# Ten x tiles loaded at once, wv and the last two tiles behind the fourth tile's transpose, one output add on GpSimd

## The chip, the core and the metric

The kernel runs on one core of a Trainium2 chip. The core has TensorE (PE) with its weight loads (PEld), VectorE (DVE), ScalarE (ACT), GpSimd (POOL) and SyncE (SP), whose queue issues all DMAs of this kernel. Each engine works through its own queue in order; waits between engines are semaphores. The metric is the device time of one execution in microseconds (us), as the median of several runs.

## The reference

One block of a transformer over 2048 tokens of width 1024: attention with 32 heads of 32, and a gated MLP beside it, in bf16.

```python
xn = layernorm(x)                                   # B, S, D = 1, 2048, 1024
qkv = (xn @ wqkv) ...                               # q, k, v: 32 heads x 2048 x 32
p = softmax(einsum("bhqd,bhkd->bhqk", q, k) * 32 ** -0.5)
s = (p @ v, heads side by side) @ wo
y = layernorm(xn)
h = gelu(y @ w1 + b1)                               # width 3584
g = silu(h @ w2 + b2)
out = x + s * g
```

## The kernel before

**Planning.** The kernel doesn't emit its instructions as it goes. It adds each as an operation with an engine, an expected duration, a priority and the buffers it reads and writes to a plan; `_Plan.run` then plays the plan through in expected time and so fixes the order on each engine, and `settle` derives the semaphore waits. The order is static: what the chip does sooner or later than expected doesn't change it. For a DMA, `rate`, `occ` and `lat` are the expected GB/s, ns of issue and ns of landing, and work on them only through that order.

**Prologue.** x is read in 16 tiles of 128 tokens (`load_x`, line 641, buffers `xst`). For each tile VectorE takes batch statistics (L852, two halves; L854 puts them together; tiles 1 and 3 go over ScalarE, L838), GpSimd takes the power -1/2 (L861) and `normalize` (L808) writes the normalized tile to `gw`. Tiles 0 to 3 and 5 are transposed on TensorE (`tr_item`, L794, copied by ScalarE, L798), all others by a DMA transpose from SP (L814), so that `xnT` holds the normalized x with its width on the partitions. From `xnT` TensorE makes Q and K of the first head group (`q_item`, `k_item`, `qk_item`; weights `wqk`; cast by VectorE at L752, L765, L742) and V (`v_half`, weights `wv`, cast at L730). `load_v` (line 654) reads wv, 512 KB, where an x tile has 256 KB.

**Scores.** A unit is a pair of key tiles by 256 queries by the four heads of a group: eight matmuls (L915) into four of six PSUM banks, then two exponentials of 128x1024 on ScalarE (L924). Units run through the whole kernel, their order is fixed; the first eight have the pairs (query block, key pair) (0,0), (0,1), (1,0), (1,1), (0,2), (1,2), (2,0), (2,1), then come (0,3), (1,3), (2,2), (0,4), (1,4), (2,3), (0,5), (1,5), (0,6), (1,6), (0,7), (1,7). So unit 5 needs K of tiles 4 and 5, unit 9 of tiles 6 and 7, unit 12 of 8 and 9, unit 15 of 10 and 11. Between units TensorE does the projections, the MLP and the products with V ("dense" work). Where it has none ready, the plan fills in matmuls on the identity (L694).

**The end.** The output projection of the last block of 256 tokens is done in four parts of 128 tokens by 512 columns, i2 = 0 to 3 (lines 1446 to 1510); `fin` marks this block. Its first seven head groups are summed early and kept in fp32 (`xf`); the last group's part is multiplied by the gate (L1499), added to `xf` (L1506 for i2 = 0, 1, 2; i2 = 3 goes another way, L1494 to L1503), and stored (L1509, four stores from SP in the order of i2). i2 = 0 and 1 belong to the last but one tile of tokens, 2 and 3 to the last tile, whose quotient (L1286 to L1296) comes after its last exponentials.

**Queue of SP in the prologue:** x0 to x3, two wqk, x4 to x9, wv, x10, x11, four small b1 loads, transpose of tile 4, x12, x13, transposes of tiles 6 to 9, x14, x15, transposes of tiles 10 to 15.

Of the kernel before, what the change touches and what calls it, by code (L numbers as in the profile page):

```python
# [7 lines left out]
ALU = mybir.AluOpType  # L8
# [459 lines left out]
def bass_recurrent_scan__mha_block__mixer_channel_mlp__prompt_kernel(  # L468
# [14 lines left out]
    HG, DC, NT, FB = 8, D // 128, S // 128, F // 128  # L483
# [16 lines left out]
    with ExitStack() as st:  # L500
        def sb(name, shape, dt):
            return st.enter_context(nc.sbuf_tensor(name, list(shape), dt))
# [11 lines left out]
        xnT = sb("xnT", [128, DC, S], BF16)  # L514
# [47 lines left out]
        xnb = [gw[:, i * 1024:(i + 1) * 1024] for i in range(4)]  # L562
# [15 lines left out]
        def c_f32(n):  # L578
            return 67 + 1.0417 * n
# [4 lines left out]
        def c_b4(n):  # L584
            return 67 + 0.2605 * n
# [9 lines left out]
        def linked(o, item):  # L595
            d = item.chunks[-1]
            if d not in o.deps:
                o.left += 1
                d.users.append(o)
            o.deps[d] = True  # L600
            item.evacs.append(o)

        def dve(fn, occ, R, W, prio, item=None, extra=()):
            o = add("DVE", fn, occ, DL, R, W, prio, extra=extra)
            if item is not None:
                linked(o, item)
            return o

        def act(fn, occ, R, W, prio, item=None):
            o = add("ACT", fn, occ, AL, R, W, prio)  # L610
            if item is not None:
                linked(o, item)
            return o

        def pool(fn, occ, R, W, prio=3):
            return add("POOL", fn, occ, PL, R, W, prio)

        def dma(sem, fn, nbytes, R, W, prio=3, extra=(), rate=290.0, occ=430, lat=2500.0):
            return add("SP", fn, occ, lat, R, W, prio, sem=sem, nbytes=nbytes, extra=extra, rate=rate)
# [18 lines left out]
        def fl3(t):  # L638
            return t[:].rearrange("p u j q -> p (u j q)")

        def load_x(t, extra=()):
            dma(f"x{t}", lambda e: e.dma_start(xst[t], x2[t * 128:(t + 1) * 128, :]), 262144, [], [XS(t)],
                rate=390.0, prio=2, occ=500, lat=2450, extra=extra)
# [10 lines left out]
        def load_v(pr, extra=()):  # L654
            src = A_wqkv[:, 2 * D + pr * 256: 2 * D + (pr + 1) * 256].rearrange("(c p) n -> p c n", p=128)
            dma("wv", lambda e: e.dma_start(wv[:], src), 524288, [], [("wv",)], prio=2, rate=200.0, extra=extra)
# [8 lines left out]
        load_x(7)  # L665
        load_x(8)
        load_x(9)
        load_v(0)
        load_x(10)
        load_x(11)  # L670
        pool(lambda e: e.memset(b1c, 0.0), 150, [], [("b1c", k) for k in range(4)], 0)
        for k in range(4):
            dma(f"b1{k}", lambda e, k=k: e.dma_start(b1c[32 * k:32 * k + FB, :], B_b1.rearrange("(q b p) -> b q p", b=4, p=32)[k]),
# [132 lines left out]
        first, trs = {}, {}  # L806

        def normalize(t, rs):  # L808
            def nf(e):
                return e.tensor_scalar(xnb[t % 4], xst[t], mv[:, t, 0:1], lnp[:, t, 1:2], op0=ALU.subtract, op1=ALU.mult)  # L810
            rw = ([XS(t), ("mv", t), rs], [("xnb", t % 4)], 1)
            first[t] = pool(nf, 0, *rw) if t in PN else dve(nf, c_b4(1024) + 118, *rw)
            if t >= NTR and t not in TRP:
                trs[t] = dma(f"tr{t}", lambda e: e.dma_start_transpose(xnT[:, :, t * 128:(t + 1) * 128], xnb[t % 4]), 262144,  # L814
                    [("xnb", t % 4)], [("xnT", t, c) for c in range(DC)], prio=0, rate=300.0, occ=1300, lat={4: 3000, 6: 1600}.get(t, 1000))

        def after(tokens, of):

# [6 lines left out]

        for n in range(NPR):
            if n == 3:
                load_x(12, [first[4]])
                load_x(13, [first[4]])
            if n == 4:  # L830
                load_x(14, [first[7]])
                load_x(15, [first[7]])
            groups = [(2 * n,), (2 * n + 1,)] if n < 2 else [(2 * n, 2 * n + 1)]
            for ts in groups:
                if ts[0] in AT:
                    a_ = ts[0]
                    for k, f, sc in ((0, ACT.Copy, 1.0 / D), (1, ACT.Square, D ** -0.5)):
                        act(lambda e, k=k, f=f, sc=sc, a_=a_: e.activation(  # L838
                            fl3(PA[a_ // 2])[:, k * 1024:(k + 1) * 1024], xst[a_], f, scale=sc, accum_out=mv[:, a_, k:k + 1]),
                            c_acts(1024) + 93, [XS(a_)], [("st", a_, k)], 1)  # L840
                    dve(lambda e, a_=a_: e.tensor_tensor(lnp[:, a_:a_ + 1, 2], mv[:, a_:a_ + 1, 0], mv[:, a_:a_ + 1, 0], op=ALU.mult), 65,
                        [("st", a_, 0)], [("s2", a_)], 0.95)
                    dve(lambda e, a_=a_: e.scalar_tensor_tensor(lnp[:, a_:a_ + 1, 0], mv[:, a_:a_ + 1, 1], EPS, lnp[:, a_:a_ + 1, 2],
                                                                op0=ALU.add, op1=ALU.subtract), 65,
                        [("st", a_, 1), ("s2", a_)], [("ve", a_)], 0.95)
                    dve(lambda e, a_=a_: e.tensor_tensor(mv[:, a_:a_ + 1, 1], mv[:, a_:a_ + 1, 1], lnp[:, a_:a_ + 1, 2], op=ALU.subtract),
                        65, [("st", a_, 1), ("s2", a_)], [("mv", a_)], 1.1)
                for t in ts:
                    if t in AT:
                        continue  # L850
                    for c in range(2):
                        dve(lambda e, t=t, c=c: e.bn_stats(stats[:, t, c, :], xst[t][:, c * 512:(c + 1) * 512]),  # L852
                            605, [XS(t)], [("st", t, c)], 1.2)
                    dve(lambda e, t=t: e.bn_aggr(mv[:, t, :], stats[:, t, :, :].rearrange("p c s -> p (c s)")),  # L854
                        110, [("st", t, 0), ("st", t, 1)], [("mv", t)], 0.95)
                lo, hi = ts[0], ts[-1] + 1
                rs = ("rs", lo)
                if ts[0] not in AT:
                    dve(lambda e, lo=lo, hi=hi: e.tensor_scalar_add(lnp[:, lo:hi, 0], mv[:, lo:hi, 1], EPS), 80,
                        [("mv", t) for t in ts], [("ve", lo)], 0.95)  # L860
                pool(lambda e, lo=lo, hi=hi: e.tensor_tensor(lnp[:, lo:hi, 1], lnp[:, lo:hi, 0], mhalf[:, lo:hi], op=ALU.pow),  # L861
                     500, [("ve", lo), ("mhalf",)], [rs], 0)
                for t in ts:
                    normalize(t, rs)
            if n < NTR // 2:
                plan.dense["tr"] += [tr_item(2 * n), tr_item(2 * n + 1)]
            pro_q += [tr_item(t) for t in (2 * n, 2 * n + 1) if t in TRP]
            if n == 0:
                pro_q.append(qk_first())
            else:  # L870
                if n < NG0:
                    pro_q.append(q_item(n))
                pro_q.append(k_item(n))
            pro_q.sort(key=lambda it: it.pos)
            if n % 2 and n > 1:
                if n == 3:
                    q0_q.append(q_item(3, "q0", 6.0))
                else:
                    q0_q.append(qk_item(0, 0, n // 2, wq0, (0.5, 14.0, 28.0)[n // 2 - 1]))
                q0_q[-1].due = 16 * (n // 2) + (8 if n == 3 else 0)  # L880
# [478 lines left out]
        for w in range(HG):  # L1359
# [24 lines left out]
            for qb in range(NQB):  # L1384
# [44 lines left out]
                for t2 in range(2):  # L1429
                    tb = 2 * qb + t2  # L1430
                    ri = tb % 3 if tb < 12 else tb - 9
# [9 lines left out]
                    xr, gr = xg[:, 0:1024], xg[:, 1024:2048]  # L1441
# [4 lines left out]
                    for nh in range(2):  # L1446
                        late = qb >= NQB - 2
                        fin = qb == NQB - 1
                        it = _Item("wo", 64 * 7 + 8 * qb + 4 * t2 + 2 * nh)
                        i2 = 2 * t2 + nh  # L1450
                        sl_ = slice(nh * 512, (nh + 1) * 512)
# [29 lines left out]
                        xk = (qb, i2)  # L1481
                        xf = (gw if fin else w1_flat)[:, i2 * 1024:(i2 + 1) * 1024].bitcast(F32)
# [19 lines left out]
                        if whole:  # L1502
                            dve(lambda e, xr=xr, gr=gr, sl_=sl_: e.tensor_tensor(xr[:, sl_], gr[:, sl_], xr[:, sl_], op=ALU.add),  # L1503
                                c_b16(512), [("gr", ri, nh)], [("xr", ri, nh)], -1 + 0.1 * i2)
                        else:
                            dve(lambda e, xr=xr, gr=gr, sl_=sl_, xf=xf: e.tensor_tensor(xr[:, sl_], gr[:, sl_], xf, op=ALU.add),  # L1506
                                c_f32(512), [("gr", ri, nh), ("xf", xk)], [("xr", ri, nh)], -1 + 0.1 * i2 if fin and t2 else 2.05 if fin else 1)
                        if fin:
                          dma(f"osl{i2}", lambda e, xr=xr, tb=tb, sl_=sl_: e.dma_start(  # L1509
                            out2[tb * 128:(tb + 1) * 128, sl_], xr[:, sl_]), 131072, [("xr", ri, nh)], [], prio=0, rate=390.0, lat=1000.0)  # L1510
# [70 lines left out]
```

## Time and profile before

| | |
|---|---|
| median of 3 runs | 1029.0 us (1028.65 to 1030.27) |
| profiled execution, its own time | 1029.85 us |
| its span, first to last instruction | 1028.1 us |
| granted TensorE clock, mean | 0.998 |
| ScalarE exponentials L924 | 988, 920.4 us busy |
| HBM | 146.55 MB read, 12.06 MB written |

The profile is one execution, seen by the hardware profiler. Its page gives busy times by engine, the chain of work that ended last, followed back from the end, and groups of instructions with what ended the idle time before them. Answers to queries of the trace give who waited for whom, a timeline of any stretch, and DMAs with their time to landing. In timeline lines the columns are start, length, engine, line, operation, output and input, count, and in brackets idle time before and what ended it.

DMAs of the prologue, from the trace: x0 to x3 are issued from 0.73 us, wqk from 2.59, x4 to x9 from 4.08, wv at 8.41 (landing 7.7 us later), x10 and x11 from 8.88 (7.9 us), b1 from 10.43, the transpose of tile 4 at 14.99 (3.6 us), x12 and x13 from 16.40, the transposes of tiles 6 to 9 from 20.67, x14 and x15 from 26.02, the transpose of tile 10 at 28.20.

### The profile page before, as it was taken

What the parts mean: (1) busy time and instruction counts of PE and PEld (TensorE: products, weight loads), DVE (VectorE), ACT (ScalarE), POOL (GpSimd) and SP (SyncE); (2) the same over time, 40 slices, a digit from 0 to 9 for tenths busy, and PEclk for the clock granted to TensorE, in tenths of its full rate; (3) what the DMA queues carried; (4) which work ended last, traced back from release to release, by engine and by line L of the source; (5) the groups of instructions that cost most, each with busy time, mean ns of one, the idle gap of its engine ahead of it and who ended that gap; (6) DMA issues with size and microseconds to landing.
All of it is one profiled execution on the core that took longest, in us unless ns stands there. A gap on an engine that the chain in (4) does not pass through costs nothing.

```text
span 1028.1 us, 31991 instructions
## 1 busy us (share of the span) xinstructions
PE 1002.5 (98%) x14354; PEld 636.9 (62%) x14354; DVE 957.0 (93%) x1367; ACT 1015.9 (99%) x1086; POOL 12.5 (1%) x22
## 2 busy tenths in 40 slices
PE   8999999999999999999999999999999999999997
PEld 7656666666666576667665666666666665664443
DVE  8999999899989999998899989998999889978987
ACT  8999999999999999999999999999999999999997
POOL 2200000000000000000000000000000000000000
PEclk9999999999999999999999999999999999999999
DMA  8667843766664767537556576674365753874321
GB/s 226 132 166 213 196 128 83 200 175 174 183 193 136 202 179 220 130 103 202 150 148 191 146 215 172 163 196 142 88 150 161 222 163 88 267 237 123 108 92 64
DMA packets 313714, 167.77 MB, mean 163 GB/s; under 512 B 52200, under 2 KB 301544, under 8 KB 313576
## 3 DMA queue, kind: packets, MB, share of 16 engines
q1 hardware_dynamic: 313576, 165.71, 58.0%
q8 instruction: 113, 1.85, 0.8%
q14 instruction: 25, 0.20, 0.1%
HBM read 146.55 MB, written 12.06 MB: 154 GB/s over the span
## 4 chain that ended last, share of the span: by engine, by line
ACT 89%; PE 5%; DVE 3%; DMA 2%; issue 0%; SPq 0%; POOL 0%
ACT P L924 81%; ACT ut L1138 4%; PE ps L633 3%; ACT gw L1166 1%; DMA w2r<-in_B_w_dram 1%; ACT P L1262 1%; DVE stats L852 1%; PE ps L915 1%; PE ps L628 1%; ACT w1r L924 1%; ACT w2r L924 1%; DMA hT<-in_A_x_dram 1%; DMA xnT<-gw 0%; ACT hT L924 0%; DVE gw L810 0%
## 5 line engine op out<-in xcount | busy, mean ns | idle before, releaser
L924 ACT ACTIVATE P<-ps 128x1024 bf16<-128x1024 f32 x988 | 920.4, 1229 | 1.3 <-PE ps L915 1.3
L941 DVE TENSOR_TENSOR PA<-P 128x2048 bf16<-128x2048 bf16 x173 | 209.9, 1216 | 24.7 <-ACT P L924 23.9
L633 PE MATMUL ps<-w2r,hT 128*128 128x256 bf16 x1792 | 224.0, 273 | 4.0 <-DMA w2r<-in_B_w_dram 1.8
L633 PE MATMUL ps<-yT,w1r 128*128 128x256 bf16 x1792 | 227.5, 273 | 0.3 <-DVE QKT L742 0.3
L955 DVE TENSOR_TENSOR PR<-PR,PA 128x2048 bf16<-128x2048 bf16 x173 | 209.6, 1211 | 1.3
L915 PE MATMUL ps<-QKT 32*128 32x256 bf16 x4032 | 200.2, 273 | 8.4 <-ACT P L924 6.4
L633 PEld LDWEIGHTS ps<-w2r,hT 128*128 128x128 bf16 x1792 | 163.2, 98 | 54.4 <-issue 30.2
L633 PEld LDWEIGHTS ps<-yT,w1r 128*128 128x128 bf16 x1792 | 164.1, 98 | 52.6 <-issue 29.3
L915 PEld LDWEIGHTS ps<-QKT 32*128 32x128 bf16 x4032 | 59.8, 92 | 137.5 <-ACT P L924 130.0
L628 PE MATMUL ps<-P,V 128*32 128x256 bf16 (+1 forms) x4080 | 136.8, 272 | 0.0
L633 PE MATMUL ps<-xnT,wqk 128*128 128x512 bf16 (+2 forms) x584 | 131.3, 354 | 1.8 <-DVE gw L1159 1.0
L628 PEld LDWEIGHTS ps<-P,V 128*32 128x32 bf16 x4080 | 95.7, 96 | 31.2 <-issue 21.6
L633 PE MATMUL ps<-wv,xnT 128*128 128x256 bf16 (+2 forms) x704 | 87.8, 264 | 1.7 <-DMA xnT<-gw 1.7
L633 PEld LDWEIGHTS ps<-xnT,wqk 128*128 128x128 bf16 x584 | 49.6, 98 | 51.4 <-issue 14.6
L1107 DVE TENSOR_TENSOR hT<-ps,b1T 128x512 bf16<-128x512 f32 x112 | 76.7, 684 | 4.6 <-PE ps L633 4.2
L941 DVE TENSOR_TENSOR PR<-P 128x2048 bf16<-128x2048 bf16 x60 | 72.9, 1214 | 0.8 <-ACT P L924 0.8
L633 PEld LDWEIGHTS ps<-wv,xnT 128*128 128x128 bf16 x704 | 55.8, 98 | 24.5 <-issue 10.3
L1138 ACT ACTIVATE ut<-ut 128x3072 bf16<-128x3072 bf16 (+2 forms) x27 | 59.1, 2190 | 0.0
L1010 DVE STREAM_TRANSPOSE nt<-ps 128x256 f32<-128x256 f32 x63 | 27.9, 444 | 13.7 <-PE ps L628 13.7
L742 DVE CAST QKT<-ps 128x512 bf16<-128x512 f32 x58 | 39.7, 684 | 0.8 <-PE ps L633 0.3
L1132 DVE TENSOR_TENSOR ut<-hT 128x2048 bf16<-128x2048 bf16 (+1 forms) x37 | 35.3, 957 | 0.2
L1141 DVE TENSOR_TENSOR hT<-ut,hT 128x2048 bf16<-128x2048 bf16 (+1 forms) x37 | 35.0, 952 | 0.0
(118 smaller groups left out, 587.7 us busy)
## 6 DMA issues: line engine op xcount, KB each, us to landing
w1r<-in_B_w_dram SPq DMA_DIRECT2D x112, 512.0 KB, 4.4
w2r<-in_B_w_dram SPq DMA_DIRECT2D x128, 448.0 KB, 4.6
yst<-in_A_x_dram SPq DMA_DIRECT2D x18, 256.0 KB, 4.2
wqk<-in_A_wqkv_dram SPq DMA_DIRECT2D x16, 256.0 KB, 3.4
g_scratch<-gw SPq DMA_DIRECT2D x32, 128.0 KB, 3.8
hT<-in_A_x_dram SPq DMA_DIRECT2D x14, 256.0 KB, 4.1
o_scratch<-ot SPq DMA_DIRECT2D x56, 64.0 KB, 3.6
xnT<-o_scratch SPq DMA_DIRECT2D x7, 512.0 KB, 6.4
```

The costliest lines, as they stand in the source:

```text
L628: ins = e.matmul(dst(j), lhsT=lhsT(j), rhs=rhs(j), start=start, stop=stop, tile_position=(0, 32 * j), skip_group_check=True)
L633: return e.matmul(dst, lhsT=lhsT, rhs=rhs, start=start, stop=stop, skip_group_check=True)
L742: dve(lambda e: e.tensor_copy(QKT[sl][:, which, tq * 512:(tq + 1) * 512], bank(it.bank)), c_ps(512), [], [(nm, sl, 2 * tq), (nm, sl, 2 * t ...
L915: ins = e.matmul(bank(b0[j], kk * 256, (kk + 1) * 256), lhsT=QKT[sl][32 * j:32 * j + 32, 1, kb * 128:(kb + 1) * 128], rhs=QKT[sl][32 * j:3 ...
L924: x = act(lambda e, h=h: e.activation(Pt[pi][:, 2 * h:2 * h + 2].rearrange("p j k q -> p (j k q)"), ps[:, pr[h] * 1024:(pr[h] + 1) * 1024] ...
L941: return dve(lambda e: e.tensor_tensor(dst[:].rearrange("p u j q -> p (u j) q"), src[:].rearrange("p u j k q -> p (u j) k q")[:, :, 0, :], ...
L955: return dve(lambda e: e.tensor_tensor(fl3(pr), fl3(pr), fl3(PA[i]), op=ALU.add), c_b16(2048), [("PA", i), tok], [tok], 3.2)
L1010: dve(lambda e: e.transpose(nt_t[:], bank(pv.bank, 256, 512)), c_ps(256) + 120, [], [("nt",)], prio, pv)
L1107: w1_ev[p] = dve(lambda e: e.tensor_tensor(hT[:, hs], bank(it.bank).rearrange("p (k t) -> p k t", k=2), b1T[:, 2 * pi:2 * pi + 2].unsqueez ...
L1132: dve(lambda e, u_=u_, x_=x_: e.tensor_tensor(u_, x_, x_, op=ALU.mult), c_b16(n), hs_, [("ut", ui)], gp)
L1138: act(lambda e: e.activation(ua, ua, ACT.Tanh, scale=GC), c_acts(run * 512), uts, uts, ga)
L1141: dve(lambda e, u_=u_, x_=x_: e.tensor_tensor(x_, u_, x_, op=ALU.mult), c_b16(n), [("ut", ui)] + hs_, hs_, gp)
```

## The change

x10 to x13 are loaded right behind x9; wv, x14 and x15 are loaded behind the normalization of tile 4 (on SP that is behind its transpose); the expected landing times of three transposes are changed, which works on the planned order alone; and the add of the output part i2 = 1 of the last block goes to GpSimd.

```diff
         load_x(9)
-        load_v(0)
         load_x(10)
         load_x(11)
+        load_x(12)
+        load_x(13)
...
-                    ..., prio=0, rate=300.0, occ=1300, lat={4: 3000, 6: 1600}.get(t, 1000))
+                    ..., prio=0, rate=300.0, occ=1300, lat={4: 1500, 6: 2400, 7: 1600}.get(t, 1000))
...
         for n in range(NPR):
             if n == 3:
-                load_x(12, [first[4]])
-                load_x(13, [first[4]])
-            if n == 4:
-                load_x(14, [first[7]])
-                load_x(15, [first[7]])
+                load_v(0, [first[4]])
+                load_x(14, [first[4]])
+                load_x(15, [first[4]])
...
                         else:
-                            dve(lambda e, ...: e.tensor_tensor(xr[:, sl_], gr[:, sl_], xf, op=ALU.add),
-                                c_f32(512), [("gr", ri, nh), ("xf", xk)], [("xr", ri, nh)], -1 + 0.1 * i2 if fin and t2 else 2.05 if fin else 1)
+                            fa = lambda e, ...: e.tensor_tensor(xr[:, sl_], gr[:, sl_], xf, op=ALU.add)
+                            rw = [("gr", ri, nh), ("xf", xk)], [("xr", ri, nh)]
+                            if fin and i2 == 1:
+                                pool(fa, 1500, *rw)
+                            else:
+                                dve(fa, c_f32(512), *rw, -1 + 0.1 * i2 if fin and t2 else 2.05 if fin else 1)
```

What the planned orders of the two builds show:

- ScalarE: the same order throughout.
- SP: wv, x14 and x15 between the transposes of tiles 4 and 6, and then the transposes of tiles 6 to 15 in a row; one later store and one w1 load change places; the second of the last four stores waits for GpSimd.
- TensorE: from unit 4 to unit 20 the dense work stands otherwise between the same units. K's matmuls of tiles 4 and 5 begin in front of unit 4 instead of behind it; the V matmuls that wait for tile 10 stand behind unit 11 instead of in front of it, with four matmuls of tile 11, in front of unit 12. 30 and 6 fillers instead of 42 and 8. Behind unit 20 two groups change places, then all is the same.
- VectorE: between the normalizations of tiles 6 and 15 casts of K and Q stand earlier and the normalizations of tiles 6 to 13 later among the statistics; in the end one add fewer.
- GpSimd: one add more, its last instruction.

More of the change, by code (lines that the diff above doesn't have):

```diff
@@ L814, in normalize @@
                 trs[t] = dma(f"tr{t}", lambda e: e.dma_start_transpose(xnT[:, :, t * 128:(t + 1) * 128], xnb[t % 4]), 262144,
-                    [("xnb", t % 4)], [("xnT", t, c) for c in range(DC)], prio=0, rate=300.0, occ=1300, lat={4: 3000, 6: 1600}.get(t, 1000))
+                    [("xnb", t % 4)], [("xnT", t, c) for c in range(DC)], prio=0, rate=300.0, occ=1300, lat={4: 1500, 6: 2400, 7: 1600}.get(t, 1000))
         def after(tokens, of):
@@ L1505, in bass_recurrent_scan__mha_block__mixer_channel_mlp__prompt_kernel @@
                         else:
-                            dve(lambda e, xr=xr, gr=gr, sl_=sl_, xf=xf: e.tensor_tensor(xr[:, sl_], gr[:, sl_], xf, op=ALU.add),
-                                c_f32(512), [("gr", ri, nh), ("xf", xk)], [("xr", ri, nh)], -1 + 0.1 * i2 if fin and t2 else 2.05 if fin else 1)
+                            fa = lambda e, xr=xr, gr=gr, sl_=sl_, xf=xf: e.tensor_tensor(xr[:, sl_], gr[:, sl_], xf, op=ALU.add)
+                            rw = [("gr", ri, nh), ("xf", xk)], [("xr", ri, nh)]
[3 more added lines that the diff above has]
+                                dve(fa, c_f32(512), *rw, -1 + 0.1 * i2 if fin and t2 else 2.05 if fin else 1)
                         if fin:
```

## The prediction

> **What bounds the kernel now.** First the page's busy times, then who ScalarE waited for, as its busiest engine.
>
> ```profile
> PE 1002.5 (98%) x14354; PEld 636.9 (62%) x14354; DVE 957.0 (93%) x1367; ACT 1015.9 (99%) x1086; POOL 12.5 (1%) x22
> ```
>
> ```profile
> engine line waited for: us in total, times, longest us
> ACT PR L1494 <- PE ps L633: 3.0, 1, 3.0
> ACT PA L838 <- DMA hT<-in_A_x_dram: 2.1, 1, 2.1
> ACT P L924 <- PE ps L915: 1.3, 3, 0.6
> ACT hT L924 <- PE ps L915: 0.8, 1, 0.8
> ACT L679 <- PEq L1566: 0.7, 1, 0.7
> ACT xnT L798 <- PE ps L794: 0.6, 2, 0.3
> ```
>
> ScalarE is the bound: 1015.9 of 1028.1 us busy, and its order of instructions is the same in both builds. So the time can fall only by its idle 12.2 us: 8.5 us in these rows, and 3.6 us after its last instruction (1024.47 to 1028.1). The timeline dates the rows: 0.34 us at 12.35, 0.22 us at 22.11 and 0.85 us at 34.06; of the other two in the third row, 0.65 us ends at 198.61 and 0.5 us lies between 280 and 290; 3.0 us is the tail. The first 12 us (start, x1's load) hold instructions that the change leaves where they are.
>
> The 0.85 us is explained by the chain of waits, in order of time (start, length, what):
>
> ```profile
> 27.76 0.44 DVE gw L810 x2
> 28.20 4.82 DMA xnT<-gw
> 33.02 0.05 issue
> 33.06 0.62 PE ps L633 x8
> 33.68 0.36 PE ps L915 x8
> 34.04 0.02 issue
> 34.06 1.94 ACT hT L924 x2
> ```
>
> Tile 10's DMA transpose (issued 28.20) lands 4.8 us later; TensorE waits with eight V matmuls (L633) for it, and behind these in its queue stands a score unit (L915, eight matmuls that feed two exponentials), which needs no tile 10. I call the units u1, u2, ... : this is u11. The DMA view of single stretches shows what a transpose takes otherwise; the first line is tile 6's (issued 20.67), the second tile 10's, each with its us to landing:
>
> ```profile
> xnT<-gw SPq DMA_TRANSPOSE x1, 2.7
> ...
> xnT<-gw SPq DMA_TRANSPOSE x1, 4.8
> ```
>
> Tile 10's has x14 and x15 in front of it (issued 26.02 and 26.5; median to landing 4.7 us).
>
> The 0.22 us, in the timeline:
>
> ```profile
> 21.18 0.42 DVE L765 CAST QKT<-ps 128x256 bf16<-128x256 f32 x1
> ...
> 21.66 0.40 PE L915 MATMUL ps<-QKT 32*128 32x256 bf16 x8
> ...
> 22.11 3.77 ACT L924 ACTIVATE P<-ps 128x1024 bf16<-128x1024 f32 x4 [0.22 <-PE ps L915]
> ```
>
> u5 waits for K of tiles 4 and 5 to be cast; units follow each other by 1.83 us, so 19.32 (u4) + 1.83 = 21.15 was its turn. It came 0.5 us late and cost 0.22; u11 came 1.27 us late (33.62 for 32.35) and cost 0.85. So a unit may be late by 0.3 to 0.4 us for nothing.
>
> The tail, in the timeline:
>
> ```profile
> 1020.78 1.28 DVE L1506 TENSOR_TENSOR hT<-hT,gw 128x512 bf16<-128x512 bf16 x2
> ...
> 1021.25 0.40 PE L628 MATMUL ps<-P,ones 128*32 128x128 bf16 x16
> ...
> 1021.98 0.31 DVE L1286 STREAM_TRANSPOSE nt<-ps 128x128 f32<-128x128 f32 x1
> ```
>
> TensorE's last row sums end at 1021.65; the transpose L1286 that opens the last quotient begins only at 1021.98, behind the two adds. From there to the last add (L1503, to 1025.86) and its store (issued 1025.89, landing in 1.7 us) each step waits for the one before.
>
> **The change, part by part.** *Loads.* On SP, x10 to x13 take the places of wv (8.41), x10 and x11 (8.88 to 10.39). The bytes are equal, 1 MB, so what lies behind starts as before: the four b1 loads, and tile 4's transpose at 14.99, which waits for VectorE. wv goes from 8.41 to 16.40, behind that transpose (1.35 us of issue), past x10, x11 and b1; x14 and x15 follow it, instead of x12 and x13 (landed by 21.5) and instead of 26.02. Issue costs 0.43 to 0.58 us each on a queue that is then free until tile 6's transpose. In flight from 16.4 are 1 MB, where it was 0.5 MB; the 18.0 to 19.7 stretch moved some 300 GB/s, so they are through near 21.5, and tile 6's transpose moves data only from about 22. After them no load precedes a transpose until the sixteenth. wv's landing isn't shown there: the three wv loads of the trace took 5.2 to 7.7 us, thus 21.6 to 24.1. In the new order the first V matmul comes behind u6 (21.15 + 1.83), at 23.3; I take 22 (only wv's own bytes and half of x14 share the way), cost nothing, and keep 24.1, which makes u7 0.7 us late, a stall of 0.35.
>
> *TensorE's order.* Four of K's matmuls for tiles 4, 5 now stand in front of u4, the rest behind it: 19.65 + 4 x 0.11 + 0.27 puts the end near 20.2 instead of 21.15. VectorE's order puts this cast in front of tile 6's normalization (both would begin at 20.2), so u5 keeps its turn at 21.15: **0.22 us gained**. Price: they wait for tile 4's transpose (14.99 + 3.6 = 18.6), and so does u4. Their turn is 18.67, after 30 filler matmuls, and u4's 19.32, so this hides.
>
> The same order lets u11 pass before the wait for tile 10; u12 now stands behind it and four matmuls of tile 11. VectorE reaches tile 10's normalization later, by one batch statistic and its moved casts: adding rows (statistic 0.60, aggregate 0.11, normalization 0.45, cast 0.33, V cast 0.65), 20.2 + 7.8 = 28.0 for K of tiles 6, 7, then the normalization ends at 29.0 instead of 28.2. At 2.8 us a transpose (1.31 apart) tile 10 lands at 31.9, tile 11 at 33.2. u12's turn is 32.1 + 1.83 = 33.95; twelve V matmuls at 0.055 are through at 33.4. **0.85 us gained.** u9 needs the cast that ends at 28.4 to 28.5, turn 28.47: within the tolerance. The later units: K of tiles 12, 13 is wanted near 38.9 and tile 13 lands near 38.3; tiles 14, 15 land near 40 and 41, wanted at 41.6. VectorE's statistics and normalizations end about 1 us sooner (37.4 for 38.5), so its tree adds don't hold the gain back. From u20 on all orders are the same and the 1.07 us shift everything.
>
> *Tail.* One add (0.64 us on VectorE) goes to GpSimd. L1286 then begins when the row sums are there, 1021.70: **0.28 us gained**. The trace has no such add on GpSimd. Below: 0.24 us, a multiply of 16 columns (L888). Above: L890's 0.277 us times 512/16, 8.9 us. Nearest by kind of slope are a memset of 32 columns (0.124 us) and an iota of 128 (0.239): 1.2 ns a column and stream; two reads and a write of 512 columns give 1.8, with a start of 0.1 some 2.0 us, which I take. It begins near 1020.95, when L1499 has ended, and ends by 1023. Its store now stands in SP's queue in front of the last two; the third is ready at 1024.8, the last at 1025.6, so anything below 3.8 us costs nothing.
>
> The Trainium skill (SBUF — State Buffer, "Who interferes with whom") says that a VectorE instruction with two SBUF inputs and a GpSimd instruction that reads SBUF exclude each other, and that the later one waits for the other's end. The 16-column multiply L894 took 0.54 us under VectorE's adds, twice L890's 0.28, as that rule has it. By it GpSimd would begin behind the add that VectorE keeps (it starts 0.17 us earlier), at 1021.45, and the sum stays. The Trainium skill (GPSIMD Engine Reference, 3.1) gives some 2.6 cycles at 1.2 GHz a column, by estimate 1.1 us plus dispatch: the sum would be the same.
>
> Sum: 0.22 + 0.85 + 0.28 = 1.35 us. The profiled run took 1029.85, span 1028.1 and 1.75 around it: 1026.75 and 1028.5 after. It lay 0.85 above the median of the runs shown, so the median goes from 1029.0 to **1027.65**.
>
> **The rivals.** *B: the waits in mid-kernel go too.* The 0.65 us at 198.61 comes from a w2 load that took 6.67 us (median 4.6), the 0.5 us from one of 5.91. For: both are single slow landings among 128, and a shifted kernel may meet other traffic. Against: TensorE's progress releases these loads, so they shift along. 1027.65 - 1.15 = 1026.5.
>
> *C: the stall moves.* If tile 10 still takes 4.8 us, u12 comes at 34.7, 0.75 late, stall 0.4; or wv lands at 24.1, stall 0.35; or u9's cast is late. Against: nothing is loaded near tile 10. 1028.0 to 1028.4.
>
> *D: slower, by GpSimd.* If the add costs in proportion to its columns, it ends at 1020.95 + 8.9 = 1029.85; the last store issues two places of 0.36 us later, 1030.7, lands 1.7 us on, and the end (0.5 us behind landing) is 1032.9: 4.8 us later than before, less 1.07, gives +3.7, 1032.7. It decides from 3.8 us for the add. For: the power of 16 columns (L892) took 3.29 us. Against: L888's 0.24 is mostly start.
>
> *E: slower, by tile 4.* If wv, x14 and x15 hold up tile 4's transpose for all their 1 MB (3.5 us at 300 GB/s), u4 and VectorE's cast come 3.4 us late, a stall of 3.0; less 1.35 that is +1.65, 1030.65. It decides from 0.6 us of delay. For: this transpose took 3.6 us, 0.9 over tile 6's, with x12 and x13 behind it. Against: they are issued after it, as x14 was after tile 9's, which took 2.8.
>
> **How the numbers follow.** Forecast 0.44; B 0.28; C 0.07; D 0.13; E 0.08. What this kernel's measurement can tell from no change is about 0.2%, 2.06 us; its runs spread over 1.6 us, so I let 0.12 of the forecast's 0.44 measure faster than that. Faster 0.12 + 0.28 = 0.40; E lies 0.4 us from the bound and is halved: same 0.32 + 0.07 + 0.04 = 0.43; slower 0.13 + 0.04 = 0.17. The range 1026.0 to 1030.0 leaves out D and E; the forecast alone spans 1026.8 to 1028.5.
>
> **What would show it.** Right: no ScalarE wait at 22 and 33 to 35; tile 10's transpose near 2.8 us; wv landed before 23.3; K of tiles 4, 5 cast near 20.2; L1286 0.05 us behind the row sums; one GpSimd add of 1 to 3 us ending before the third store. Wrong: a wait for wv or tile 4 on TensorE before u7, a ScalarE wait at u9 or u12, the last store waiting for GpSimd, or other waits than two between 100 and 1000 us.

## The result and the profile after

| | before | after |
|---|---|---|
| median of 21 runs each | 1029.65 us (1028.35 to 1030.81) | 1031.32 us (1029.59 to 1033.44) |
| ratio, 95% interval | | 1.0015 [1.0009, 1.0021] |
| profiled execution, its own time | 1029.85 us | 1032.37 us |
| its span | 1028.1 us | 1030.6 us |

The changed kernel is slower by 1.67 us; 1027.65 had been forecast. Its profiled execution lies 1.05 us above its median, so the profiles differ by more (2.5 us) than the medians. The span is best cut at three places on ScalarE, the engine that sets the pace: its first exponential of the scores, the 45th (by then all 16 tiles are in), and the end of its last ones. All are read from the timeline.

| stretch, us | before | after | difference |
|---|---|---|---|
| start to the first exponential | 13.27 | 13.66 | +0.39 |
| first to 45th exponential | 42.60 | 42.82 | +0.22 |
| 45th to the last exponentials' end | 964.99 | 965.09 | +0.10 |
| from there to the end (the tail) | 7.21 | 9.01 | +1.80 |

So the loss lies in the last 9 us, and the stretch of 45 exponentials at the beginning, where 1.07 us were to be gained, gained nothing.

**The tail.** The page's busy times of the kernel after, and then the waits of TensorE and SP in the last 12 us of it (who waited, for whom: us in total, times, longest):

```profile
PE 1002.0 (97%) x14340; PEld 635.5 (62%) x14340; DVE 956.4 (93%) x1366; ACT 1016.5 (99%) x1086; POOL 15.0 (1%) x23
```

```profile
PE ps L628 <- issue: 1.7, 1, 1.7
...
SPq L1512 <- POOL hT L1505: 0.7, 1, 0.7
```

TensorE stood still 1.7 us in the row sums (L628), which is the hole of the sections below, and "issue" says that nothing the profile follows released it. The timeline of the kernel after shows the place:

```profile
1021.50 0.68 DVE L1505 TENSOR_TENSOR hT<-hT,gw 128x512 bf16<-128x512 bf16 x1
...
1021.66 1.54 POOL L1505 TENSOR_TENSOR hT<-hT,gw 128x512 bf16<-128x512 bf16 x1 [978.27 <-DVE hT L1498]
...
1022.02 0.39 PE L628 MATMUL ps<-P,ones 128*32 128x128 bf16 x15
...
1024.16 0.22 PE L628 MATMUL ps<-P,ones 128*32 128x128 bf16 x1 [1.75 <-issue]
1024.41 0.32 DVE L1285 STREAM_TRANSPOSE nt<-ps 128x128 f32<-128x128 f32 x1 [2.23 <-PE ps L628]
```

15 of the last 16 row sums are through at 1022.41; the sixteenth starts at 1024.16. The transpose that opens the last quotient (L1285, before L1286) needs it, and VectorE, free since 1022.18, waits. GpSimd's add ends at 1023.20, before the sixteenth row sum starts; experiment 4 takes it out. What ran meanwhile is in the DMA view of 1021.2 to 1022.8 (queue, kind: packets, MB, share of 16 engines):

```profile
q8 instruction: 1, 0.02, 5.5%
```

By its name and its count this queue brings TensorE's own instructions. In the whole kernel it shows 112 packets with 1.84 MB, 16 KB each; 14340 matmuls and as many weight loads over 112 make 256 instructions a packet. This packet started at 1021.31 and took 1.40 us, and the sixteenth row sum started 2.85 us after it was begun. So the border between two blocks of instructions seems to lie in front of the last row sum; the experiments test that. The kernel before has a packet at 1022.00, while TensorE waits 1.6 us for VectorE in any case. The change moved the border, since it plans 14 filler matmuls fewer, 30 and 6 for 42 and 8 near 17 and 22 us: 28 instructions.

**The prologue.** ScalarE's waits of the kernel after, from 12 us to 60 us:

```profile
ACT P L923 <- PE ps L914: 0.5, 1, 0.5
ACT w1r L923 <- PE ps L914: 0.4, 1, 0.4
...
```

The waits of 0.22 and 0.85 us at u5 and u11 are gone. In their place stand 0.45 us at 35.57, which is u12, and 0.37 at 45.34. The timeline shows that u5's gain is real:

```profile
20.57 0.42 DVE L766 CAST QKT<-ps 128x256 bf16<-128x256 f32 x1
...
21.52 0.40 PE L914 MATMUL ps<-QKT 32*128 32x256 bf16 x8
```

K of tiles 4 and 5 is cast at 20.57, 0.6 us earlier than before, and u5 (21.52) follows on its turn. The chain of waits of the kernel after, from its piece at 30.52 us on, shows what holds u12 and u17:

```profile
30.52 4.23 DMA xnT<-gw
...
34.79 0.40 PE ps L633 x4
...
39.33 4.53 DMA xnT<-gw
43.86 0.05 issue
43.90 1.06 PE ps L633 x12
```

These are the transposes of tile 11 and of tile 15. Tile 10's is slow too, in the DMA view of its issue at 29.24:

```profile
xnT<-gw SPq DMA_TRANSPOSE x1, 4.5
```

It took 4.8 us before, and now x14 and x15 are no longer on their way with it (they landed at 22.2 and 22.8). So it is slow without them. In both traces a packet of TensorE's instructions starts in the transpose: at 29.55 in the kernel before (tile 10 issued 28.20, tile 11 29.48), at 30.25 after (29.24, 30.52).

### The profile page after: what moved, and what is told of

The parts are those of the page before. It is cut to its first block, busy times and chain, and to the rows that moved or that the text cites. A ratio compares the mean times of both kernels' runs of the same rounds, so it can differ in the third digit from the quotient of the medians.

```text
span 1030.6 us, 31965 instructions
## 1 busy us (share of the span) xinstructions
PE 1002.0 (97%) x14340; PEld 635.5 (62%) x14340; DVE 956.4 (93%) x1366; ACT 1016.5 (99%) x1086; POOL 15.0 (1%) x23
## 3 DMA queue, kind: packets, MB, share of 16 engines
q8 instruction: 112, 1.84, 0.8%
## 4 chain that ended last, share of the span: by engine, by line
ACT 83%; PE 8%; DVE 5%; DMA 3%; issue 1%; POOL 0%; SPq 0%
ACT P L923 76%; PE ps L633 5%; ACT ut L1137 4%; DMA w2r<-in_B_w_dram 2%; PE ps L914 1%; PE ps L628 1%; DVE stats L851 1%; ACT gw L1165 1%; ACT P L1261 1%; DMA xnT<-gw 1%; DVE gw L811 1%; DVE PA L940 1%; DVE PR L954 1%; ACT w2r L923 1%; DMA hT<-in_A_x_dram 0%
## 5 line engine op out<-in xcount | busy, mean ns | idle before, releaser
L633 PEld LDWEIGHTS ps<-yT,w1r 128*128 128x128 bf16 x1792 | 164.1, 98 | 52.6 <-issue 29.3
L628 PE MATMUL ps<-P,V 128*32 128x256 bf16 (+1 forms) x4080 | 136.8, 272 | 0.0
L628 PEld LDWEIGHTS ps<-P,V 128*32 128x32 bf16 x4080 | 95.7, 96 | 31.0 <-issue 21.2
```

The costliest lines, as they stand in the source:

```text
L628: ins = e.matmul(dst(j), lhsT=lhsT(j), rhs=rhs(j), start=start, stop=stop, tile_position=(0, 32 * j), skip_group_check=True)
L633: return e.matmul(dst, lhsT=lhsT, rhs=rhs, start=start, stop=stop, skip_group_check=True)
```

## The experiments

What was open: does the place of the block borders of TensorE's instructions make the hole in the tail and the slow transposes, or do the moved loads, the new order or the add? Fillers compute nothing, so a few more or fewer of them, in time in which TensorE waits, should move the borders and little else (a matmul and its weight load are two instructions). That no longer holds where all of them go, as kernels 7 and 8 show. In the edits below `nfil["m"]` counts the fillers as they are emitted, one or two at a time; by 25 us the changed kernel has 100, the one before 114, and both have eight more, two at 875 us and six near 1013. Ratios are against the kernel before in the same series.

**1. The changed kernel with the 14 fillers put back**

```diff
         def filler(e, b, n):
+            nfil["m"] += n
+            if nfil["m"] == 100:
+                n += 14
```

> The changed kernel with 14 more filler matmuls in its second filler group behind unit 5 (20 instead of 6; TensorE is idle 0.9 us there), so that TensorE's stream is again as long as before the change. Theory 1, the place at which TensorE's instructions are fetched: the changed kernel loses 1.75 us in a hole of TensorE at 1022.41, one matmul before its last row sum, because a 16 KB block of its instructions (fetched from 1021.31) is not there yet; 14 matmuls fewer in the prologue put the block's border there. With them back the hole goes, the last quotient's transpose begins within 0.1 us of the row sums, and the kernel is 1.6 to 2.2 us faster than the changed one, about 0.2 us under the kernel before. Theory 2, GpSimd's add holds up the end (its reads or its store): the hole stays at 1.5 us or more and the time stays 1.5 us above the kernel before. Theory 3, the later start of 0.4 us and slower prologue are the change's own: whatever the tail does, ScalarE's last exponential ends 0.5 us or more later than in the kernel before.

Measured: 1029.79 us, ratio 1.0000 [0.9991, 1.0009], 1.5 us below the changed kernel's first median. No hole; from the last exponentials to the end 6.95 us, against 9.01 in the changed kernel and 7.21 before. 14 matmuls on the identity, 22 us into the kernel, move what happens a thousand microseconds later, and the loss is gone. Its last exponentials do end 0.7 us later than in the profile before, as theory 3 said, but the start and the middle stretch that make this up vary by more than that between profiles (below), so theory 3 is left open.

**2. The kernel before with 14 fillers fewer**

```diff
+            if 64 < nfil["m"] <= 92:
+                n -= 1
```

> The kernel before, with 14 filler matmuls fewer (28 instead of 42 behind unit 3), nothing else changed. Theory 1 (border of the instruction block): a hole of 1 to 2 us appears in TensorE's stream inside the last row sums, with a 16 KB fetch ending 1 to 1.5 us before its end, and the kernel is 1.5 to 2.3 us slower. Theories 2 and 3: nothing in the tail changes, the time stays within 0.3 us.

Measured: 1030.25 us, ratio 1.0002 [0.9993, 1.0011], no hole, 7.21 us. The expected hole didn't come. Counting the instructions on TensorE's queue tells why: this kernel has two semaphore instructions less than I had allowed for, and the border falls one instruction behind the last row sums, where TensorE waits for VectorE anyway (its next matmul starts 2.7 us after the fetch began).

**3. and 4. One part of the change alone.** The kernel before with the GpSimd add and nothing else; the changed kernel without it.

> The kernel before with the GpSimd add alone. Theory 1: TensorE's stream is as before, no hole; the last quotient's transpose begins 0.05 us behind the row sums instead of 0.33 and the kernel is 0.2 to 0.3 us faster. Theory 2: a hole or a late last store, 1 us slower or more.

> The changed kernel without the GpSimd add (loads and expected landings alone). Theory 1: the hole of 1.75 us is there as in the changed kernel; 1.5 to 2.2 us slower than the kernel before. Theory 2: no hole, the time of the kernel before within 0.4 us. On the prologue: transposes of tiles 10, 11, 14 and 15 land in 4 us or more wherever a 16 KB fetch of TensorE's instructions falls into their flight, and in 2.7 to 2.9 where none does, in all four runs of this call.

Measured: the add alone 1030.17 us, ratio 1.0004 [0.9995, 1.0013], tail 7.07; the rest alone 1030.99, ratio 1.0009 [1.0000, 1.0017], tail 8.39 with a hole of 1.3 us. The hole belongs to the part that changes the fillers, not to the add. The add takes 1.53 us here and is worth 0.14 us of tail: the last quotient's transpose begins 0.04 us behind the row sums, as expected, but these end 0.14 us later behind the last exponentials. The median doesn't show the 0.2 to 0.3 us that were expected of it, and the rest alone is 1.1 us slower than the kernel before, not 1.5 to 2.2. Of the transposes of tiles 10, 11, 14 and 15 in these four profiles the 12 with a packet in their flight took 3.5 to 4.6 us, the four without 2.8 to 2.9.

**5. to 8. Other borders.** The changed kernel with one filler fewer (`if nfil["m"] == 100: n -= 1`), the kernel before with 13 fewer (`if 64 < nfil["m"] <= 90: n -= 1`), and both without about 50 (`n = 0` where 32 < m <= 46 or 64 < m <= 100; in the kernel before where 64 < m <= 114).

> The changed kernel with one filler matmul fewer (5 instead of 6 behind unit 5). Counted from TensorE's stream (a matmul is two instructions, 256 instructions are a 16 KB block), the border of the block that holes the changed kernel lies behind the 255th of the 256 instructions of the last row sums; one matmul fewer puts it behind them, in front of the last two output matmuls, which wait 1.6 us for VectorE anyway. Theory 1 (border): the hole in the row sums is gone, the tail (last exponential's end to the end) is 6.9 to 7.3 us instead of 9.0, the time 1.2 to 1.9 us below the changed kernel's. Theory 2 (something else in the tail): one filler matmul changes nothing, tail 9 us. Theory 4, the gain of the run with 14 more fillers came from the prologue or by chance: as theory 2.

> The kernel before with 13 filler matmuls fewer (29 instead of 42), where 14 fewer did nothing: its border now lies just where the changed kernel's does, one instruction in front of the end of the last row sums. Theory 1: a hole of 1.2 to 1.8 us in front of the last row-sum matmul, tail 8.2 to 9.0 us instead of 7.2, 1.0 to 1.8 us slower than the kernel before. Theory 2: tail 7.2 us, no change, since loads and the GpSimd add are those of the kernel before.

> The changed kernel with 50 filler matmuls fewer (all 36 behind units 3 and 5 and 14 of the first 46), which moves the fetches of TensorE's instructions later by some 3 us: from 30.25 to about 33.5, behind the flight of tiles 10 and 11, and from 39.87 to 42 or later, behind tiles 14 and 15. Theory 5, a fetch in flight is what makes DMA transposes late: tiles 10, 11, 14 and 15 land in 2.7 to 3.0 us; a tile that meets the fetch near 33.5 (12) or near 25 (8, 9) lands in 3.5 to 4.8; ScalarE's stalls between units 11 and 18 go, from the first exponential to the 45th 41.0 to 41.7 us instead of 42.8; the tail is 6.9 to 7.3. In all 2 to 3 us faster than the changed kernel and 0.7 to 1.5 faster than the kernel before. Rival, the transposes of tiles 10 and 11 are late by their place (behind a pause of SP's queue): they stay at 4 us or more.

> The kernel before with its 50 filler matmuls behind units 3 and 4 left out, loads as before (x14 and x15 right in front of tile 10's transpose). Theory 5: the fetch moves from 29.55 to about 32.5 to 33.5 and tiles 10 and 11 land in 2.7 to 3.0 us though the two loads stand in front of them; ScalarE's stall of 0.85 at unit 11 goes; 0.7 to 1.3 us faster than the kernel before. Rival (the prediction's reason, x14 and x15 hold the transposes up): they stay at 4.4 to 4.8 us and the stall stays.

| kernel | us | ratio, 95% interval | 1st to 45th exponential | tail | hole in the last row sums |
|---|---|---|---|---|---|
| after, 1 filler fewer | 1028.88 | 0.9989 [0.9981, 0.9998] | 41.76 | 7.36 | none |
| before, 13 fewer | 1031.14 | 1.0017 [1.0008, 1.0025] | 43.30 | 7.91 | 0.77 |
| after, 50 fewer | 1030.45 | 1.0013 [1.0003, 1.0024] | 43.94 | 6.95 | none |
| before, 50 fewer | 1030.89 | 1.0009 [1.0001, 1.0018] | 43.30 | 7.22 | none |

One filler fewer takes the hole out of the changed kernel, and 13 fewer put it into the kernel before, which has no other part of the change; its timeline:

```profile
1021.58 0.39 PE L628 MATMUL ps<-P,ones 128*32 128x128 bf16 x15
...
1022.74 0.22 PE L628 MATMUL ps<-P,ones 128*32 128x128 bf16 x1 [0.77 <-issue]
```

As in the changed kernel, 15 row sums lie in front of the border and one behind it. The hole is smaller than expected (0.77 us for 1.2 to 1.8), and the kernel 1.5 us slower, as expected. Counted in the traces, with its semaphore instructions, TensorE's last row-sum matmul is the 28,866th instruction in all four profiles with a hole (the two of the changed kernel, the one without the add, and this one) and in none of the nine others. For the tail this settles the cause.

In kernels 7 and 8 the tail is good and the prologue bad, which I had not expected. Their third packet of instructions starts at 33.18 and 33.08 instead of near 30, and the second at 24.50 and 23.23 instead of 19 to 22. The slow transposes moved along: tiles 10 and 14 take 2.7 to 2.8 us, tile 11 4.4 and 4.5, and tiles 7 and 8 of the one and 6 of the other, 2.7 to 3.7 us in the other profiles, are now at 4.2 to 4.5. The kernel without 50 fillers that is otherwise the kernel before still loads x14 and x15 right in front of tile 10; the DMA view of its tile 10, issued at 29.3:

```profile
xnT<-gw SPq DMA_TRANSPOSE x1, 2.7
```

These loads land at 29.75 and 30.40, in the first 1.1 us of its flight. That speaks against the loads as the cause by itself. It also speaks against the rival, a place behind a pause of SP's queue, which tiles 10 and 14 have here as before. The first loss of these kernels, at u5, is something else. Stretches of the changed kernel without 50 fillers (stretch, its length, PE busy and its matmuls, granted clock, DMA share, GB/s):

```profile
17.00:18.90 1.90, 0.89 (x12) 1.00 0.72 203
18.90:21.50 2.60, 2.60 (x16) 0.52 0.72 258
```

Without the 30 fillers that fill the wait for tile 4, TensorE stands idle, is then granted 0.52 of its clock, and needs 2.7 us for the twelve matmuls of K and Q that take the changed kernel 1.5. u5 comes with a wait of 0.93 us. The fillers do their work, and taking them out is no way to move a border.

**9. to 11. Does it hold?** One filler fewer once more, the changed kernel beside it, and a few fillers fewer in each late group (`if nfil["m"] > 94: n -= 1`). The last edit takes out seven and not the six of its expectation: three at 22 us, one at 875 and three at 1014, so the border moves by 14 instructions.

> The changed kernel with one filler matmul fewer, run once more, beside the changed kernel itself, to see whether the first result (1028.88 us, ratio 0.9989) holds. Border theory: the last block border of TensorE's instruction stream again lies behind the last burst of row sums, so the tail (end of the last exps to the end) stays near 7.2 us and the median stays 0.5 to 1.0 us below the kernel before, near 1028.9. Rival (the first result was the luck of one stretch of runs): median within 0.3 us of the kernel before, or no further from the changed kernel than 1 us.

> The changed kernel unchanged, in the same call as the version with one filler fewer. Border theory: hole of 1.3 to 1.8 us in TensorE's last burst of row sums and a tail near 8.4 to 9.0 us again, median 1.3 to 1.9 us above the kernel before and 1.8 to 2.6 us above the version with one filler fewer. Rival (chance of the stretch): no hole, median within 0.5 us of the kernel before.

> The changed kernel with six filler matmuls fewer, all six from the last group (u9 to u11), so the border falls 12 instructions further behind the last burst. Border theory: no hole, tail 7.0 to 7.4 us; the prologue decides the rest: the third fetch of TensorE's instructions starts about as in the changed kernel or a little later, so tile 10 or 11's transpose takes 4 us or more and the median lies between 1028.5 and 1030. Rival (the tail depends on the number of fillers by way of the clock or TensorE's queue, not by the border): a tail as in the changed kernel, median near 1031.

| kernel | us | ratio, 95% interval | 1st to 45th exponential | tail | hole in the last row sums |
|---|---|---|---|---|---|
| after, 1 filler fewer, again | 1029.51 | 1.0003 [0.9994, 1.0012] | 42.02 | 7.41 | none |
| after, again | 1030.23 | 1.0011 [1.0003, 1.0020] | 41.86 | 8.55 | 1.40 |
| after, 7 fewer | 1028.80 | 1.0001 [0.9992, 1.0009] | 42.48 | 6.94 | none |

The holes are as expected: one in each profile of the changed kernel, none in the versions with fewer fillers. The medians are not. One filler fewer lies 0.72 us below the changed kernel where I expected 1.8 to 2.6, and no longer below the kernel before; that is what the rival said, so the first result was at least in part luck. The changed kernel lies 0.81 above the kernel before, not 1.3 to 1.9. Seven fewer lie 1.43 below the changed kernel and by their ratio level with the kernel before. So no version here is shown to beat the kernel before. With one filler fewer the tail is also 0.4 us longer than with seven: the border has only gone on by two instructions, behind the first of the last two weight loads of the output. That load starts 1.9 us after the fetch began, and the second one waits, as the timeline of kernel 9 shows:

```profile
1023.05 0.10 PEld L633 LDWEIGHTS ps<-yst,xnT 128*128 128x128 bf16 x1 [0.40 <-issue]
```

The prologue differs between profiles of the same kernel: 42.82 and 41.86 us for the changed one. Its second profile has no ScalarE wait behind tile 10, and there tile 10 took 3.6 us and tile 11 2.8, with the packet 0.47 us behind tile 10's issue, instead of 1.01 us. A few tenths decide whether a packet meets a transpose. I therefore counted all transposes of the 13 profiles (11 each), by whether a packet of instructions was in flight with it:

| | transposes | us to landing, lowest, median, highest |
|---|---|---|
| a packet begun at least 0.5 us before the landing and ended at least 0.5 us after the issue | 49 | 2.9, 4.2, 5.4 |
| no such packet | 94 | 2.7, 2.8, 3.6 |

Of the 94, nine took over 3.0 us, five of them tile 4 with x tiles loading beside it. That a packet slows a transpose is an association over 143 of them, with borders shifted on purpose in eight of the profiles; how it does so no trace shows, as one packet moves only 16 KB. One part of the delay can be placed: SP takes 1.23 to 1.36 us to issue a transpose in 119 cases and 1.59 to 2.70 in the other 24, and in each of these 24 a packet was in flight during the issue.

## Why the prediction was wrong

**What bounds the kernel, and the GpSimd add: right.** ScalarE's order and busy time are the same (1016.5 us for 1015.9). The add took 1.54 us for an estimate of 2.0, ended at 1023.20, 4.4 us before the third store was issued, and rival D did not come. The Trainium skill (SBUF — State Buffer, "Who interferes with whom") has the later of a VectorE instruction with two SBUF inputs and a GpSimd instruction that reads SBUF wait; here VectorE's add kept its 0.68 us, and GpSimd's 1.54 holds 0.52 us of overlap, so the trace neither shows nor excludes that wait.

**0.28 us in the tail: the step that failed worst.** "L1286 then begins when the row sums are there, 1021.70" took it as given that the row sums come when they came before. They came 1.75 us later by their own engine, which cost 1.80 us instead of a gain. Where no hole stands, the step holds at half to nearly all of its size: 0.14 us with the add alone and 0.26 with the fillers put back. The prediction has no term for the 14 fewer fillers: its 30 fillers in front of u4 stand there as time that hides. The 28 instructions fewer move every later block border, here into the last row sums.

**0.22 us at u5: right.** The cast started at 20.57, later than the 20.2 named (the sum written there, 19.65 + 4 x 0.11 + 0.27, gives 20.36, and everything ran 0.4 us later from the start on), and u5 ran on its turn.

**wv behind tile 4: right, and rival E did not come.** wv landed 21.5 us into the kernel for an estimate of 22, and tile 4's transpose landed at 18.7, in time for u4. The bounds were read from too few rows: the trace has four such wv loads, of 4.4 to 7.7 us, not three of 5.2 to 7.7, and this one took 4.7. x14 and x15 landed at 22.2 and 22.8, not near 21.5.

**0.85 us at tile 10: wrong in its cause.** "Tile 10's has x14 and x15 in front of it" named the wrong neighbour (x15, by the way, was issued at 26.64, not 26.5), and so "at 2.8 us a transpose tile 10 lands at 31.9" didn't follow. It landed at 33.8 and tile 11 at 34.7. What came is rival C as written, "if tile 10 still takes 4.8 us, u12 comes at 34.7, 0.75 late, stall 0.4": 4.5 us, a stall of 0.45. A second stall, 0.37 us behind tile 15, stood in no rival. The order did let u11 pass, and whether u12 then waits goes with tile 10: in the four profiles of the new order in which tile 10 took 3.3 to 3.7 us there is no wait at u12 (41.76 to 42.24 us to the 45th exponential), in the three in which it took 4.5 to 4.7 u12 waits 0.4 to 0.6 us. But the old order came to 41.92 as well, in the kernel with the add alone, so that the new order gains anything on the whole isn't shown. Over all profiles with the fillers near their old number it lies between 41.76 and 42.82, the old one between 41.92 and 43.30.

By term, for the profiled pair: forecast -0.22 - 0.85 - 0.28; measured in the prologue +0.22, in the tail +1.80. The start's +0.39 and the middle's +0.10 make up the rest of 2.5 us; neither was followed further, and over the 13 profiles, whatever the kernel, the start varies between 12.68 and 13.98 us and the middle between 964.04 and 966.18. The tail tells the kernels apart: 6.94 to 7.41 us without a hole in the row sums, 7.91 to 9.01 with one.

## What to carry to other kernels

An instruction that computes nothing and hides in idle time still has a place in its engine's instruction stream: when an edit changes their number, look where the border of the last block falls, and whether a chain that sets the end waits there. Before a slow transfer is put down to the loads issued ahead of it, look for every queue that is busy in its time, the instruction queues too, and see whether a transfer without them is fast. A single profile is no measure of a stretch whose stalls hang on such meetings; here two profiles of one kernel differ by 0.96 us over 45 exponentials.

## What the runs showed of the hardware

- A burst can outrun TensorE's instruction fetch. Over the kernel an instruction comes every 36 ns (1030.6 us for 28,680), and in the second profile of the changed kernel 104 blocks begin between 60 and 1019 us, while ScalarE waits 0.25 us there in all. In the last burst 123 instructions went by in 1.1 us after the fetch began, and the first instruction of the next block started 2.3 to 2.85 us after the beginning of its fetch in the four profiles with a hole. The Trainium skill (Runtime: NRT & Kernel Launch, "Instruction fetch mechanics") gives blocks of 256 instructions and calls the crossing "mostly hidden": the size agrees, and so does "mostly", but the one border in the burst held TensorE up for 1.75 us.
- A DMA transpose of 256 KB with a 16 KB packet of instructions in flight took 4.2 us in the median, 2.8 without.
- In the changed kernel without 50 fillers, after 1.1 and 0.6 us of idle (between 16.4 and 18.6 us), TensorE was granted 0.52 of its clock over the next 2.6 us, 0.50 over 2 us in the other kernel without these fillers.
- GpSimd's add of 128x512 took 1.53 to 1.54 us, VectorE's 0.68 for the same.
